# Local and summary attention with two dense layers on one core: queries and keys loaded as token pairs and turned by 64-column products with the identity

## Chip, cores and metric

One Trainium2 chip, one core of it. The metric is the device time of one launch in microseconds (us); lower is better. Before the change: 624.55 us, the median of three runs (623.58 to 625.62).

## What is computed

An attention over 2 batches, 8 heads, 768 tokens and 64 dimensions, in float32, whose result is the input of two dense layers. Cut to what matters:

```python
k_sum = k.reshape(B, H, nb, 32, D).max(axis=3)      # maximum over blocks of 32 tokens
v_sum = v.reshape(B, H, nb, 32, D).mean(axis=3)
scores_l = scale * q @ k.T, masked to |i - j| < 16
scores_s = scale * q @ k_sum.T + log(32)
a = softmax(concat(scores_l, scores_s))
x = a @ concat(v, v_sum)                             # then (B*S, H*D) = (1536, 512)
x = softplus(x @ w1_in) @ w1_out                     # 512 -> 2048 -> 512
out = relu(x @ w2_in) ** 2 @ w2_out
```

## The kernel before

**Tiling.** The tokens are cut into 12 tiles of 128, six of each batch. For a tile the kernel needs the queries and keys with the head dimension on the partitions: `qT` and `kT` hold two heads on the 128 partitions (head 2p on 0 to 63, head 2p+1 on 64 to 127), four such pairs and then the tokens. They come from `ld_qk` (line 336), which loads a unit of 256 tokens, all heads, with tokens on the partitions, and `tr` (line 344), which turns it. A unit is two halves r of 128 tokens. For each half there is one load of 256 KB, one PSUM bank that takes four transposes of 128x128 (one for each pair of heads, line 351), a copy of the bank to `kT` or `qT` by ACT or DVE (lines 296 and 298), and for keys a maximum by DVE from the same bank into `ks` (line 359). There are 3 units of keys and 3 of queries in a batch, so 24 loads and 24 banks in all. The word bank is used below for such a filled bank and its work.

**Attention of a tile.** POOL copies the 96 keys of a window behind the 24 block maxima (`kaug`, line 411), PE forms the scores (line 443, 64x64 corners of the array), DVE, ACT and POOL do the softmax, PE transposes the weights (line 499) and multiplies by the values (line 513, products with 64 columns and 120 rows of weights); two passes split the result into `xh` and `xl` (lines 522 and 523). The block means of the values are a product with a selection matrix (line 391, 24 columns).

**Dense layers.** All products are of float32 split in a high and a low part: three products each (lines 616 and 653). The first four of 16 chunks of the first layer are done during the attention, in steps of 256 tokens ("phase A", 24 steps); all else follows in steps of 512 tokens ("phase B"). Weights come as 64-bit floats and are put together by ACT, DVE and POOL (lines 561 to 575) in four places `raw`.

**Order.** `Plan.run` (line 86) simulates the program with the costs that each `op` carries and writes out the order of the instructions of every engine. `kb` is the price of a load on the queue of the DMAs. Where it sees PE idle it inserts products of the identity with itself (line 809, the function `warm`). On the chip each engine goes through its list in order.

```python
op("SP", 0.6, due, load, w=[(place, r)], kb=288)
op("PE", 0.66, due, mm, r=["id", (place, r)], w=[bk], take=bk)
op(("ACT", "DVE"), (0.62, 0.8), due, cp, r=[bk], give=bk, ...)
```

All loads are issued from SP, in one list: queries, keys, values, windows of values (line 377) and weights (lines 551 and 554).

Of the kernel before, what the change touches and what calls it, by code (L numbers as in the profile page):

```python
# [13 lines left out]
ALU = mybir.AluOpType  # L14
AX = mybir.AxisListType
# [163 lines left out]
def kernel(  # L179
# [54 lines left out]
    ident = ac.tile([128, 128], F32, name="ident")  # L234
# [7 lines left out]
    kT = ac.tile([128, NP, S + 32], F32, name="kT")  # L242
    ks = ac.tile([128, NP, NS], F32, name="ks")
    sel = ac.tile([128, VR, NS], F32, name="sel")
    vsum = ac.tile([NS, H * D], F32, name="vsum")
    qT = [ac.tile([128, NP, 256], F32, name=f"qT{i}") for i in range(2)]
    kaug = [ac.tile([128, NP, 2, NC], F32, name=f"kaug{i}") for i in range(2)]
# [6 lines left out]
    ab = [ps_a.tile([128, 512], F32, name=f"ab{i}") for i in range(2)] + hb[0:2]  # L254

    def st4(t):
        return t.rearrange("p (r h d) -> p r h d", h=H, d=D)

    pf = [part[i].rearrange("p a b -> p (a b)") for i in range(NB3)]
    PL = {("P", i, j): st4(pf[i][:, 1024 * j:1024 * j + 1024]) for i in range(NB3) for j in range(2)}  # L260
# [7 lines left out]
    for L in (1, 2):  # L268
        for ph, (f0, f1) in enumerate(PH):
            A = L == 1 and ph == 0  # L270
            n = 256 if A else 512
# [18 lines left out]
    def tt(e):  # L290
        return nc.gpsimd if e == "POOL" else nc.vector

    def copy(e, out_, in_, mul=None):

        if e == "ACT":
            nc.scalar.activation(out=out_, in_=in_, func=AF.Copy, **({} if mul is None else {"scale": mul}))  # L296
        else:
            tt(e).tensor_scalar(out=out_, in0=in_, scalar1=1.0 if mul is None else mul, scalar2=1.0,  # L298
                                op0=ALU.mult, op1=ALU.mult)
# [33 lines left out]
            nc.vector.memset(vwin[i], 0.0)  # L333


    def ld_qk(src, u, place, due):
        b, i = divmod(u, NU)
        for r in range(2):
            t0 = 256 * i + 128 * r
            op("SP", 0.6, due, lambda r=r, t0=t0: nc.sync.dma_start(  # L340
                out=PL[place][:, r], in_=src[b, :, t0:t0 + 128, :].rearrange("h t d -> t h d")),
                w=[(place, r)], kb=288)

    def tr(src, u, place, due):
        i = u % NU
        for r in range(2):
            bk = Bank()

            def mm(r=r, bk=bk):
                for p in range(NP):  # L350
                    nc.tensor.transpose(ab[bk.bank][:, 128 * p:128 * p + 128],
                                        PL[place][:, r, 2 * p:2 * p + 2].rearrange("t h d -> t (h d)"), ident)

            def cp(e, r=r, bk=bk):
                o = kT[:, :, 16 + 256 * i:16 + 256 * i + 256] if src is k else qT[u % 2]
                copy(e, o[:, :, 128 * r:128 * r + 128], ab[bk.bank].rearrange("p (a c) -> p a c", a=NP), None if src is k else scale)

            def kmax(r=r, bk=bk):
                nc.vector.tensor_reduce(out=ks[:, :, 8 * i + 4 * r:8 * i + 4 * r + 4],  # L359
                                        in_=ab[bk.bank].rearrange("p (a n t) -> p a n t", a=NP, t=32), op=ALU.max, axis=AX.X)  # L360

            op("PE", 0.66, due, mm, r=["id", (place, r)], w=[bk], take=bk)
            op(("ACT", "DVE"), (0.62, 0.8), due, cp, r=[bk], give=bk, w=[("kT", 2 * i + r)] if src is k else [("qT", u % 2, r)])
            if src is k:
                op("DVE", 0.67, due, kmax, r=[bk], give=bk, w=[("ks", 2 * i + r)])

    def ksum(x, due):
        op("DVE", 0.35, due, lambda: nc.vector.tensor_copy(
            out=kaug[x][:, :, :, 0:NS], in_=ks.rearrange("p a (o n) -> p a o n", o=1).to_broadcast([128, NP, 2, NS])),
            r=[("ks", i) for i in range(NTB)], w=[("kaug", x)])  # L370

    def ld_win(t, due):
        b, i = divmod(t, NTB)
# [32 lines left out]
    def mk_kaug(t, due):  # L406
        i = t % NTB
        for j in range(2):
            c0 = 128 * i + 64 * j
            us = sorted({min(max((c0 + d - 16) // 128, 0), NTB - 1) for d in (0, 95)})  # L410
            op("POOL", 0.55, due, lambda j=j, c0=c0: nc.gpsimd.tensor_scalar(
                out=kaug[t % 2][:, :, j, NS:], in0=kT[:, :, c0:c0 + WIN],
                scalar1=1.0, scalar2=1.0, op0=ALU.mult, op1=ALU.mult),
                r=["z"] + [("kT", u) for u in us], w=[("kw", t % 2, j)])

    def tile_sc(t, due):
        x, i, u = t % 2, t % NTB, (t // 2) % 2
# [4 lines left out]
        pe_mask = style in "mn"  # L422
# [5 lines left out]
        def scv(hh):  # L428
            return scb[:, hh, 0:NP * NC].rearrange("p (a c) -> p a c", a=NP)

        def mm():
            if pe_mask:
                for hh in range(2):
                    nc.tensor.matmul(out=scv(hh), lhsT=identb, rhs=maskb[:, var:var + 1].to_broadcast([128, NP, NC]),
                                     start=True, stop=False, skip_group_check=True)
                    for j in range(2):
                        nc.tensor.matmul(out=scv(hh)[:, :, 0:NS], lhsT=identb,
                                         rhs=logb[:, j:j + 1].to_broadcast([128, NP, NS]),
                                         start=False, stop=False, skip_group_check=True)
            for p in range(NP):  # L440
                for hh, j in ((0, 0), (1, 1), (0, 1), (1, 0)):
                    o = 128 * x + 64 * j
                    nc.tensor.matmul(out=scb[64 * j:64 * j + 64, hh, NC * p:NC * p + NC],  # L443
                                     lhsT=qT[u][64 * hh:64 * hh + 64, p, o:o + 64],
                                     rhs=kaug[x][64 * hh:64 * hh + 64, p, j], start=not pe_mask, stop=True,
                                     skip_group_check=pe_mask)
        op("PE", 1.7 if pe_mask else 1.15, due, mm, r=[("qT", u, x), ("kaug", x), ("kw", x, 0), ("kw", x, 1), "id"],
           w=[(sck, 0), (sck, 1)])
        if not pe_mask:
            for hh in range(2):  # L450
                op("DVE", 0.66, due, lambda hh=hh: nc.vector.tensor_tensor(  # L451
                    out=st[:, NP * hh:NP * hh + NP], in0=scv(hh),
                    in1=mask[:, var:var + 1].to_broadcast([128, NP, NC]), op=ALU.add),
                    r=[(sck, hh), "id"], w=[("s", y, hh)])
        halves = ((0, NP), (NP, H)) if t < 2 or pe_mask else ((0, H),)
        for h0, h1 in halves:
            n = (h1 - h0) / H
            hh = h0 // NP
# [12 lines left out]
            if pe_mask:  # L471
                op("DVE", 1.25 * n, due, lambda hh=hh, mv=mv: nc.vector.tensor_reduce(
                    out=mv, in_=scv(hh), op=ALU.max, axis=AX.X, negate=True), r=[(sck, hh)], w=mk)

                def exps(hh=hh, sv=sv, mv=mv, rv=rv):
# [4 lines left out]
                   w=sk + (rk if style == "n" else []), tab="exp")  # L480
            else:
                op("DVE", 1.25 * n, due, lambda sv=sv, mv=mv: nc.vector.tensor_reduce(out=mv, in_=sv, op=ALU.max, axis=AX.X),
                   r=sk, w=mk)
                op(("POOL", "DVE"), (1.8 * n + 0.1, 1.75 * n), due, lambda e, sv=sv, mv=mv, spread=spread: tt(e).tensor_tensor(
                    out=sv, in0=sv, in1=spread(mv), op=ALU.subtract), r=mk, w=sk)
# [3 lines left out]
                out=sv, in0=sv, in1=spread(rv), op=ALU.mult), r=rk, w=sk)  # L489
# [354 lines left out]
```

## Time and profile before

| | us |
|---|---|
| median of the runs | 624.55 |
| lowest, highest | 623.58, 625.62 |
| the profiled execution, its time | 623.45 |
| its span in the profile | 621.7 |
| PE busy | 601.9 |
| DVE, ACT, POOL busy | 309.6, 288.1, 201.2 |

The profile is of one execution. A record of PE is a product (MATMUL) or a load of the stationary operand (LDWEIGHTS); records overlap, so the distance from start to start is the time that an instruction takes from the engine, and the length of a record is longer. A float32 product leaves two MATMUL records, a transpose one. The column PEclk is the clock of TensorE that was granted: 1.00 stands for 2.4 GHz and 0.50 for 1.2 GHz. In the view by stages, "PE busy (x)" is the busy time and the number of instructions. In the timeline the parts are start, length, engine, line, operation, output and inputs, sizes, count, and in brackets the idle time ahead of it and what ended it.

### The profile page before, as it was taken

To read this page: it belongs to the slowest core of one execution; us is meant where nothing else is said; L and a number is where in the kernel's file an instruction comes from. 1 tells how busy PE (TensorE), PEld (TensorE's weight loads), DVE (VectorE), ACT (ScalarE), POOL (GpSimd) and SP (SyncE) were. 2 spreads that over 40 slices of the span, in tenths; PEclk is the share of its full clock that TensorE was granted. 3 is DMA by queue.
4 is the path that set the end of the run, shared out by engine and by line. 5 is a ranking of instruction groups with operands and counts; after the bars stand their busy time and mean duration, and the time that the engine had idled before them with its cause. 6 is when DMAs were issued, how large, how long until landed. Compare 5 with 4: busy or idle time off the path is not lost.

```text
span 621.7 us, 9362 instructions
## 1 busy us (share of the span) xinstructions
PE 601.9 (97%) x3751; PEld 505.4 (81%) x3751; DVE 309.6 (50%) x453; ACT 288.1 (46%) x512; POOL 201.2 (32%) x200
## 2 busy tenths in 40 slices
PE   7887899999999999999999999999999999999997
PEld 5776789999888888888888888888888888888885
DVE  4786898845754133742226752248432533242332
ACT  4776896775763225543337643356312332212220
POOL 4766776435750033411228540135000320000000
PEclk8999999999999999999999999999999999999999
DMA  9999722133550023430014430124000200010011
GB/s 214 270 263 265 189 52 58 55 93 114 166 182 14 1 68 102 135 103 0 1 34 130 143 101 1 34 97 126 16 0 1 68 2 0 1 51 18 17 52 67
DMA packets 68620, 51.33 MB, mean 83 GB/s; under 512 B 44512, under 2 KB 62944, under 8 KB 68576
## 3 DMA queue, kind: packets, MB, share of 16 engines
q1 hardware_dynamic: 68576, 50.73, 29.0%
q8 instruction: 29, 0.48, 0.3%
q14 instruction: 15, 0.12, 0.1%
HBM read 47.58 MB, written 3.15 MB: 82 GB/s over the span
## 4 chain that ended last, share of the span: by engine, by line
PE 85%; DVE 6%; DMA 4%; ACT 2%; SPq 2%; issue 0%; POOL 0%; DVEq 0%; ACTq 0%
PE h L616 41%; PE accp L653 23%; PE acc L653 18%; DMA raw<-in_moe_w_in_dram 2%; DMA late<-in_v_dram 2%; DVE raw L566 2%; SPq L340 1%; PE ab L513 1%; PE ab L499 1%; DVE sm L468 1%; ACT at L296 0%; DVE wil L575 0%; PE sc L443 0%; DVE ks L359 0%; DVE s L451 0%; DVE xl L523 0%
## 5 line engine op out<-in xcount | busy, mean ns | idle before, releaser
L616 PE MATMUL h<-xh,wih 128*128 128x512 f32 (+1 forms) x432 | 160.0, 370 | 0.5 <-DVE g1l L632 0.5
L616 PE MATMUL h<-xl,wih 128*128 128x512 f32 (+1 forms) x432 | 158.8, 368 | 1.1 <-DVE xl L523 1.1
L616 PE MATMUL h<-xh,wil 128*128 128x512 f32 (+1 forms) x432 | 158.8, 368 | 0.0
L566 DVE SCALAR_TENSOR_TENSOR raw<-raw 128x512 uint32<-128x512 uint32 x128 | 115.8, 923 | 47.6 <-ACT raw L561 28.2
L616 PEld LDWEIGHTS h<-xh,wih 128*128 128x128 f32 x432 | 81.4, 188 | 15.2 <-DVE g1l L632 0.9
L616 PEld LDWEIGHTS h<-xl,wih 128*128 128x128 f32 x432 | 81.3, 188 | 14.9 <-DVE xl L523 1.3
L616 PEld LDWEIGHTS h<-xh,wil 128*128 128x128 f32 x432 | 81.3, 188 | 14.0
L625 ACT ACTIVATE e<-h 128x512 f32<-128x512 f32 x48 | 28.7, 597 | 128.5 <-PE h L616 128.5
L627 DVE SCALAR_TENSOR_TENSOR h<-h,e 128x512 f32<-128x512 f32 x48 | 33.5, 698 | 107.2 <-ACT e L625 107.2
L623 ACT ACTIVATE h<-h 128x512 f32<-128x512 f32 (+1 forms) x60 | 29.7, 498 | 83.1 <-PE h L616 82.9
L298 POOL TENSOR_SCALAR wih<-raw 128x512 fp32r<-128x512 f32 x20 | 14.0, 701 | 153.2 <-PE h L616 143.9
L575 POOL TENSOR_TENSOR wol<-raw,woh 128x512 fp32r<-128x512 f32 x31 | 44.7, 1444 | 32.2 <-ACT woh L296 31.7
L561 ACT ACTIVATE raw<-raw 128x512 uint32<-128x512 uint16 x62 | 41.6, 674 | 17.5 <-DMA raw<-in_moe_w_out_dram 8.1
L575 POOL TENSOR_TENSOR wil<-raw,wih 128x512 fp32r<-128x512 f32 x31 | 42.0, 1353 | 22.8 <-ACT wih L296 21.3
L632 DVE TENSOR_TENSOR g1l<-h,g1h 128x512 fp32r<-128x512 f32 (+1 forms) x40 | 24.2, 607 | 33.9 <-ACT g1h L630 33.8
L675 DVE TENSOR_TENSOR part<-accp,part 128x512 f32<-128x512 f32 x24 | 16.0, 686 | 44.9 <-PE accp L653 44.9
L632 DVE TENSOR_TENSOR g2l<-h,g2h 128x512 fp32r<-128x512 f32 x28 | 19.3, 689 | 35.9 <-ACT g2h L630 35.7
L296 ACT ACTIVATE raw<-raw 128x512 f32<-128x512 f32 x41 | 27.5, 671 | 19.9 <-DVE raw L566 19.9
L632 DVE TENSOR_TENSOR g0l<-h,g0h 128x512 fp32r<-128x512 f32 (+1 forms) x40 | 24.1, 603 | 21.8 <-ACT g0h L630 21.6
L298 POOL TENSOR_SCALAR raw<-raw 128x512 f32<-128x512 f32 x23 | 18.8, 824 | 31.8 <-DVE raw L566 29.7
L630 ACT ACTIVATE g0h<-h 128x512 fp32r<-128x512 f32 (+1 forms) x40 | 21.4, 535 | 15.8 <-DVE h L627 15.4
L488 POOL TENSOR_TENSOR s<-s,sm 128x480 f32<-128x480 f32 (+1 forms) x16 | 22.9, 1435 | 16.2 <-DVE sm L470 12.6
(174 smaller groups left out, 1162.9 us busy)
## 6 DMA issues: line engine op xcount, KB each, us to landing
raw<-in_moe_w_in_dram SPq DMA_DIRECT2D x32, 512.0 KB, 4.4
raw<-in_moe_w_out_dram SPq DMA_DIRECT2D x32, 512.0 KB, 3.5
vwin<-in_v_dram SPq DMA_DIRECT2D x20, 192.0 KB, 4.2
part<-in_k_dram SPq DMA_DIRECT2D x12, 256.0 KB, 5.0
late<-in_v_dram SPq DMA_DIRECT2D x2, 1536.0 KB, 10.5
out_dram<-part SPq DMA_DIRECT2D x12, 256.0 KB, 2.2
part<-in_q_dram SPq DMA_DIRECT2D x10, 256.0 KB, 5.2
vwin<-in_v_dram SPq DMA_DIRECT2D x4, 160.0 KB, 5.1
```

The lines of the kernel that those rows point to most:

```text
L296: nc.scalar.activation(out=out_, in_=in_, func=AF.Copy, **({} if mul is None else {"scale": mul}))
L298: tt(e).tensor_scalar(out=out_, in0=in_, scalar1=1.0 if mul is None else mul, scalar2=1.0, op0=ALU.mult, op1=ALU.mult)
L488: op(("POOL", "DVE"), (1.8 * n + 0.1, 1.75 * n), due, lambda e, sv=sv, rv=rv, spread=spread: tt(e).tensor_tensor(out=sv, in0=sv, in1=sprea ...
L561: nc.scalar.activation(out=lo, in_=q4[:, :, 1], func=AF.Copy, scale=2.0 ** -13, bias=-4095.5 / 8192.0)
L566: nc.vector.scalar_tensor_tensor(out=lo, in0=hi, scalar=n, in1=lo, op0=how, op1=ALU.bitwise_or)
L575: op(("POOL", "DVE"), (1.4, 1.0), dv, lambda e: tt(e).tensor_tensor(out=ws[s][kl], in0=lo.bitcast(F32), in1=ws[s][kh].bitcast(F32), op=ALU ...
L616: nc.tensor.matmul(out=hview(st), lhsT=ws[s][wn][:, w_], rhs=xx[bl][:, kk, o:o + n], start=(kk == 0 and xx is xh and wn == "ih"), stop=(kk ...
L623: op("ACT", ta, due, lambda: nc.scalar.activation(out=hview(st), in_=hview(st), func=AF.Softplus), w=[H_], tab="sp")
L625: op("ACT", ta, due, lambda: nc.scalar.activation(out=e_t[st["g"] % 2], in_=hview(st), func=AF.Relu), r=[H_], w=[("e", st["g"] % 2)])
L627: op("DVE", tv, due, lambda: nc.vector.scalar_tensor_tensor(out=hview(st), in0=hview(st), scalar=0.0, in1=e_t[st["g"] % 2], op0=ALU.max, o ...
L632: op("DVE", tv, due, lambda: nc.vector.tensor_tensor(out=gview(st)[1], in0=hview(st), in1=gview(st)[0].bitcast(F32), op=ALU.subtract), r=[ ...
L653: nc.tensor.matmul(out=o, lhsT=a[:, sl], rhs=b, start=(st["first"] and c == 0 and not (A and m % 2)), stop=(st["last"] and c == 2 and not ...
```

## The change

A load now takes four of the eight heads (index z) and all 256 tokens of a unit, with tokens 2p and 2p+1 on partition p, so that 512 bytes in a row go to a partition where it was 256 bytes. The count (24) and size (256 KB) of the loads stay. PE turns a half z by eight products whose stationary operand is 64 columns of the data (one head, one of the two tokens) and whose moving operand is the identity of 128 columns; a head goes to partitions 0 to 63 or 64 to 127 of the bank. The copy out of the bank puts even and odd tokens back in turn (output in steps of two elements), and the maximum runs over two axes. The keys by which `Plan` tracks who waits for whom are now units and halves of the heads, not blocks of 128 tokens. The price `kb` of a load goes from 288 to 180; that of the PE step stays 0.66.

```diff
     def st4(t):
-        return t.rearrange("p (r h d) -> p r h d", h=H, d=D)
+        return t.rearrange("p (z a x) -> p z a x", z=2, a=NP)
...
     def ld_qk(src, u, place, due):
         b, i = divmod(u, NU)
-        for r in range(2):
-            t0 = 256 * i + 128 * r
-            op("SP", 0.6, due, lambda r=r, t0=t0: nc.sync.dma_start(
-                out=PL[place][:, r], in_=src[b, :, t0:t0 + 128, :].rearrange("h t d -> t h d")),
-                w=[(place, r)], kb=288)
+        for z in range(2):
+            op("SP", 0.6, due, lambda z=z: nc.sync.dma_start(
+                out=PL[place][:, z].rearrange("p a (r d) -> p a r d", r=2),
+                in_=src[b, 4 * z:4 * z + 4, 256 * i:256 * i + 256, :].rearrange("h (p r) d -> p h r d", r=2)),
+                w=[(place, z)], kb=180)
...
-                for p in range(NP):
-                    nc.tensor.transpose(ab[bk.bank][:, 128 * p:128 * p + 128],
-                                        PL[place][:, r, 2 * p:2 * p + 2].rearrange("t h d -> t (h d)"), ident)
+                for a in range(2):
+                    for r in range(2):
+                        for hh in range(2):
+                            o = 256 * a + 128 * r
+                            nc.tensor.matmul(out=ab[bk.bank][64 * hh:64 * hh + 64, o:o + 128],
+                                             lhsT=PL[place][:, z, 2 * a + hh, 64 * r:64 * r + 64], rhs=ident,
+                                             start=True, stop=True)
...
-                copy(e, o[:, :, 128 * r:128 * r + 128], ab[bk.bank].rearrange("p (a c) -> p a c", a=NP), None if src is k else scale)
+                copy(e, o[:, 2 * z:2 * z + 2].rearrange("p a (c r) -> p a r c", r=2),
+                     ab[bk.bank].rearrange("p (a r c) -> p a r c", a=2, r=2), None if src is k else scale)
...
-                nc.vector.tensor_reduce(out=ks[:, :, 8 * i + 4 * r:8 * i + 4 * r + 4],
-                                        in_=ab[bk.bank].rearrange("p (a n t) -> p a n t", a=NP, t=32), op=ALU.max, axis=AX.X)
+                nc.vector.tensor_reduce(out=ks[:, 2 * z:2 * z + 2, 8 * i:8 * i + 8],
+                                        in_=ab[bk.bank].rearrange("p (a r n c) -> p a n r c", a=2, r=2, n=8), op=ALU.max, axis=AX.XY)
...
-            us = sorted({min(max((c0 + d - 16) // 128, 0), NTB - 1) for d in (0, 95)})
+            us = sorted({min(max((c0 + d - 16) // 256, 0), NU - 1) for d in (0, 95)})
...
-        op("PE", 1.7 if pe_mask else 1.15, due, mm, r=[("qT", u, x), ("kaug", x), ("kw", x, 0), ("kw", x, 1), "id"],
+        op("PE", 1.7 if pe_mask else 1.15, due, mm, r=[("qT", u, 0), ("qT", u, 1), ("kaug", x), ("kw", x, 0), ("kw", x, 1), "id"],
```

Since `Plan.run` sees other prices and keys, the lists of all engines change in phase A; from the first step of phase B on PE's list is the same. The products of `warm` (line 809) go from 79 to 52. Lines behind the changed functions stand 7 lower in the file after the change.

On PE, at the start of the program: the first banks of keys (`part_68`, `part_69` are the places that the loads fill; `ab` and `h` are PSUM banks). Before:

```order
L351 MATMUL ab_141<-ident,part_68 128x128 x4
L351 MATMUL ab_142<-ident,part_68 128x128 x4
L351 MATMUL h_108<-ident,part_68 128x128 x4
L351 MATMUL h_109<-ident,part_68 128x128 x4
L351 MATMUL ab_141<-ident,part_69 128x128 x4
```

and after:

```order
L356 MATMUL ab_141<-ident,part_68 64x128 x8
L356 MATMUL ab_142<-ident,part_68 64x128 x8
L356 MATMUL h_108<-ident,part_68 64x128 x8
L356 MATMUL h_109<-ident,part_68 64x128 x8
L356 MATMUL ab_141<-ident,part_69 64x128 x8
```

The order is the same; each bank takes eight products in place of four transposes.

On PE, where the weights of the first two tiles are multiplied by the values (`vwin`) and the second unit of queries (`late`) is turned. Before:

```order
L351 MATMUL ab_142<-ident,late 128x128 x4
L513 MATMUL h_108<-at_134,vwin_130 64x64 x16
L513 MATMUL h_109<-at_135,vwin_131 64x64 x16
L351 MATMUL ab_141<-ident,late 128x128 x4
```

and after:

```order
L356 MATMUL ab_142<-ident,late 64x128 x8
L520 MATMUL h_108<-at_134,vwin_130 64x64 x16
L356 MATMUL ab_141<-ident,late 64x128 x8
L520 MATMUL h_109<-at_135,vwin_131 64x64 x16
L356 MATMUL ab_142<-ident,part_70 64x128 x8
```

Here banks stand between products that also have 64 columns; at other places they stand between products of 128 columns.

On SP, the loads from the 21st row of its list on (`part_70` from `in_k_dram` is the fifth unit of keys, `raw_77` from `in_moe_w_in_dram` the input weights of the fourth chunk). Before:

```order
L377 DMA vwin_131<-in_v_dram 96x8x64 x2
L340 DMA part_70<-in_k_dram 128x8x64
L551 DMA raw_77<-in_moe_w_in_dram 128x4x256
L340 DMA part_70<-in_k_dram 128x8x64
L554 DMA raw_78<-in_moe_w_out_dram 128x1024
```

and after:

```order
L384 DMA vwin_131<-in_v_dram 96x8x64 x2
L558 DMA raw_77<-in_moe_w_in_dram 128x4x256
L341 DMA part_70<-in_k_dram 128x4x128 x2
L561 DMA raw_78<-in_moe_w_out_dram 128x1024
```

The load of the weights moved ahead of one load of keys.

## Rows read from the trace of the kernel before

**Rows 1.** The page, part 1: busy time of each engine.
```profile
PE 601.9 (97%) x3751; PEld 505.4 (81%) x3751; DVE 309.6 (50%) x453; ACT 288.1 (46%) x512; POOL 201.2 (32%) x200
```

**Rows 2.** Stages: us, then PE, PEld, DVE, ACT, POOL busy, PEclk, DMA share, GB/s.
```profile
50.00:60.00 10.00, 6.61 (x137) 5.32 (x136) 6.45 (x12) 7.15 (x16) 5.76 (x8) 1.00 1.10 259
...
90.00:100.00 10.00, 9.04 (x119) 8.43 (x120) 9.93 (x16) 5.43 (x12) 7.24 (x7) 1.00 0.17 40
...
151.00:600.00 449.00, 449.00 (x1989) 369.92 (x1988) 193.63 (x268) 178.83 (x307) 108.26 (x91) 1.00 0.18 59
```

**Rows 3.** The page, below part 2: packets of the DMA engines by size.
```profile
DMA packets 68620, 51.33 MB, mean 83 GB/s; under 512 B 44512, under 2 KB 62944, under 8 KB 68576
```

**Rows 4.** Stages, as rows 2: loads of keys; the slow clock; the load of values.
```profile
2.00:9.00 7.00, 5.26 (x28) 3.40 (x25) 3.12 (x5) 1.99 (x5) 6.11 (x19) 1.00 1.19 222
9.40:16.00 6.60, 6.31 (x46) 4.81 (x50) 3.19 (x6) 3.35 (x7) 0.00 (x0) 0.50 1.09 272
18.00:20.00 2.00, 2.00 (x26) 1.69 (x19) 1.74 (x4) 2.00 (x9) 0.98 (x2) 1.00 1.08 397
```

**Rows 5.** Timeline of PE, the start: first and last banks, scores of tiles 0 and 1.
```profile
4.17 1.06 PE L351 MATMUL ab<-ident,part 128*128 128x128 f32 x4
...
11.86 1.94 PE L351 MATMUL h<-ident,part 128*128 128x128 f32 x8
...
14.85 1.68 PE L443 MATMUL sc<-kaug,qT 64*64 64x120 f32 x32
...
17.14 1.05 PE L443 MATMUL accp<-kaug,qT 64*64 64x120 f32 x32
```

**Rows 6.** Timeline of PE: one 64-column group and one bank among 128-column products.
```profile
29.82 2.08 PE L513 MATMUL h<-at,vwin 120*64 120x64 f32 x64
...
53.70 1.51 PE L391 MATMUL ab<-late,sel 128*24 128x128 f32 x48
...
61.65 0.28 PE L653 MATMUL accp<-g1l,woh 128*128 128x256 f32 x1
61.86 1.15 PE L513 MATMUL ab<-at,vwin 120*64 120x64 f32 x32
...
63.16 0.28 PE L616 MATMUL h<-xl,wih 128*128 128x256 f32 x1
...
64.36 0.28 PE L616 MATMUL h<-xh,wil 128*128 128x256 f32 x1
64.48 0.60 PE L351 MATMUL ab<-ident,part 128*128 128x128 f32 x4
...
65.03 0.28 PE L616 MATMUL h<-xl,wih 128*128 128x256 f32 x1
```

**Rows 7.** Timeline of PE, 25 to 73 us: waits and inserted products of the identity.
```profile
25.05 1.51 PE L391 MATMUL ab<-late,sel 128*24 128x128 f32 x48 [1.62 <-DMA late<-in_v_dram]
...
39.23 0.66 PE L351 MATMUL ab<-ident,part 128*128 128x128 f32 x4 [0.86 <-DVE ks L359]
...
55.15 0.72 PE L809 MATMUL h<-ident 128*128 128x256 bf16 x5
58.34 1.05 PE L443 MATMUL sc<-kaug,qT 64*64 64x120 f32 x32 [2.47 <-DVE s L451]
...
68.29 1.69 PE L809 MATMUL sc<-ident 128*128 128x256 bf16 x14
...
72.55 1.05 PE L443 MATMUL sc<-kaug,qT 64*64 64x120 f32 x32 [1.00 <-DVE kaug L368]
```

**Rows 8.** The chain that ended last, and the timeline of ACT, at 55 us.
```profile
47.78 7.58 DMA raw<-in_moe_w_in_dram
...
55.44 0.69 ACT L561 ACTIVATE raw<-raw 128x512 uint32<-128x512 uint16 x1 [2.72 <-DMA raw<-in_moe_w_in_dram]
```

**Rows 9.** Groups by line and shape, ACT: copies out of a bank, and a strided pass.
```profile
L561 ACT ACTIVATE raw<-raw 128x512 uint32<-128x512 uint16 x62 | 41.6, 674 | 17.5 <-DMA raw<-in_moe_w_out_dram 8.1 <-DMA raw<-in_moe_w_in_dram 7.6 <-DVE s L451 1.7
...
L296 ACT ACTIVATE kT<-ab 128x512 f32<-128x512 f32 x9 | 5.4, 598 | 7.2 <-PE ab L351 7.2
```

More of the change, by code (lines that the diff above doesn't have):

```diff
@@ L344, in tr, with mm, cp, kmax @@
     def tr(src, u, place, due):
         i = u % NU
-        for r in range(2):
+        for z in range(2):
             bk = Bank()
-            def mm(r=r, bk=bk):
-                for p in range(NP):
-                    nc.tensor.transpose(ab[bk.bank][:, 128 * p:128 * p + 128],
-                                        PL[place][:, r, 2 * p:2 * p + 2].rearrange("t h d -> t (h d)"), ident)
-            def cp(e, r=r, bk=bk):
-                o = kT[:, :, 16 + 256 * i:16 + 256 * i + 256] if src is k else qT[u % 2]
-                copy(e, o[:, :, 128 * r:128 * r + 128], ab[bk.bank].rearrange("p (a c) -> p a c", a=NP), None if src is k else scale)
-            def kmax(r=r, bk=bk):
-                nc.vector.tensor_reduce(out=ks[:, :, 8 * i + 4 * r:8 * i + 4 * r + 4],
-                                        in_=ab[bk.bank].rearrange("p (a n t) -> p a n t", a=NP, t=32), op=ALU.max, axis=AX.X)
-            op("PE", 0.66, due, mm, r=["id", (place, r)], w=[bk], take=bk)
-            op(("ACT", "DVE"), (0.62, 0.8), due, cp, r=[bk], give=bk, w=[("kT", 2 * i + r)] if src is k else [("qT", u % 2, r)])
+            def mm(z=z, bk=bk):
+                for a in range(2):
[5 more added lines that the diff above has]
+                                             start=True, stop=True)
+            def cp(e, z=z, bk=bk):
+                o = kT[:, :, 16 + 256 * i:16 + 256 * i + 256] if src is k else qT[u % 2]
+                copy(e, o[:, 2 * z:2 * z + 2].rearrange("p a (c r) -> p a r c", r=2),
+                     ab[bk.bank].rearrange("p (a r c) -> p a r c", a=2, r=2), None if src is k else scale)
+            def kmax(z=z, bk=bk):
+                nc.vector.tensor_reduce(out=ks[:, 2 * z:2 * z + 2, 8 * i:8 * i + 8],
+                                        in_=ab[bk.bank].rearrange("p (a r n c) -> p a n r c", a=2, r=2, n=8), op=ALU.max, axis=AX.XY)
+            op("PE", 0.66, due, mm, r=["id", (place, z)], w=[bk], take=bk)
+            op(("ACT", "DVE"), (0.62, 0.8), due, cp, r=[bk], give=bk, w=[("kT", i, z)] if src is k else [("qT", u % 2, z)])
@@ L364, in tr @@
             if src is k:
-                op("DVE", 0.67, due, kmax, r=[bk], give=bk, w=[("ks", 2 * i + r)])
+                op("DVE", 0.67, due, kmax, r=[bk], give=bk, w=[("ks", i, z)])
     def ksum(x, due):
@@ L369, in ksum @@
             out=kaug[x][:, :, :, 0:NS], in_=ks.rearrange("p a (o n) -> p a o n", o=1).to_broadcast([128, NP, 2, NS])),
-            r=[("ks", i) for i in range(NTB)], w=[("kaug", x)])
+            r=[("ks", i, z) for i in range(NU) for z in range(2)], w=[("kaug", x)])
     def ld_win(t, due):
@@ L413, in mk_kaug @@
                 scalar1=1.0, scalar2=1.0, op0=ALU.mult, op1=ALU.mult),
-                r=["z"] + [("kT", u) for u in us], w=[("kw", t % 2, j)])
+                r=["z"] + [("kT", u, z) for u in us for z in range(2)], w=[("kw", t % 2, j)])
     def tile_sc(t, due):
```

## The prediction

> **What bounds the kernel now.** I read the page first. PE is busy 97% of the span [rows 1], but that is an average over two stages. The view by stages shows them: from 151 to 600 us PE has no free moment (449.00 of 449.00 us), while between 50 and 60 us it is busy 6.61 of 10 us and the DMA engines are at 1.10, full [rows 2]. From 151 us on PE's list is unchanged, so the change is worth exactly what it moves the end of phase A. Phase A has limits in turn. Up to about 72 us the loads set the pace; at 90 to 100 us DVE is busy 9.93 of 10 us [rows 2]; behind that PE is full. A lead or a lag of PE's backlog at 72 us is therefore carried to the end, if DVE is not given more work. Then I read PE's timeline up to 73 us: its groups [rows 5, 6] and its waits [rows 7].
>
> **The loads.** Of 68,620 packets 44,512 are under 512 bytes [rows 3]. A load of keys or queries, 256 KB, is by the code 1024 pieces of 256 bytes. Alone on the queue such loads run at 222 GB/s [rows 4]: 262,144 bytes take 1.18 us. The values come in pieces of 1536 bytes at 397 GB/s [rows 4]. With 16 engines that is 18.4 ns and 61.9 ns for a piece; on the straight line between them 512 bytes take 27 ns, 302 GB/s, 0.87 us for a load. No row has this size, so this is an estimate; the ends are 1.18 us (nothing gained) and 0.66 us (the rate of the values). The nearest row is that of 256 bytes, so I take 0.87: 0.31 us saved on each of 24 loads, 7.4 us of a full queue.
>
> **The turning on PE.** Four transposes: from the last product ahead (64.36) to the second one behind (65.03) are 0.67 us, less two products of 0.12 (64.36 to 64.48) is 0.43 us for a bank [rows 6]. The eight products leave 16 records. Line 513 has the same form, 64 columns in two halves of the array: 32 more records cost 2.08 - 1.15 = 0.93 us, 29 ns each for 64 moving columns, so 58 ns for 128 [rows 6]. Line 391 moves 128 columns in four parts of the array: (1.51 - 0.28) / 48 = 26 ns [rows 6], so 51 ns in two parts. I take 55 ns between these ends: 0.88 us for a bank, 0.45 us more. At the slow clock both double.
>
> A change of width costs too. From 61.65 to 63.16 are 1.51 us [rows 6]; less two products of 0.12 and 0.93 us of records, 0.34 us stay, where the transposes leave none. In the list after, the 16 banks behind the start stand in twelve stretches, and six of those are alone among 128-column products; the others lean on groups that are 64 columns or narrower already. I count six times 0.3.
>
> So the 16 later banks add 16 x 0.45 + 6 x 0.3 = 9.0 us to PE. The Trainium skill, *TensorEngine Tiling (Array Packing)*, Key Properties, says that changing the tiling mode drains TensorE, which speaks against this change. The trace agrees, with the 0.34 us above. By that rule all twelve stretches would pay.
>
> **The start.** Before, the first bank begins at 4.17, the eighth (second half of the x8 group at 11.86) at about 12.7, and tiles 0 and 1 are scored from 14.85 and 17.14 [rows 5], at half clock: PEclk is 0.50 (1.2 GHz) from 9.40 to 16.00, while PE did short groups of transposes with waits for loads [rows 4]. The mask products between the end of the eighth bank (12.7 + 0.86) and 14.85 took 1.3 us at that clock. After, loads come every 0.87 us, so the eighth lands near 10. PE is now the later one: first bank at 3.9, at the slow clock (as the 1.06 us of the first group shows) 1.76 us, to 5.7; then seven banks at full clock with a hand-over, 0.9 us each, to 12.0; mask products half of 1.3, 0.65 us. Tile 0 is scored from 12.65; a group of scores is 1.05 us long at full clock [rows 5], with masks 1.7, so tile 1 begins at 14.35: **2.8 us earlier**. This takes the clock as staying at 2.4 GHz, since PE is no longer idle between banks. At 1.2 GHz from 9.4 us on, 3.6 us of that are lost.
>
> **From 25 to 73 us.** Here the 9.0 us must fit. PE's timeline has eleven bracketed waits, from 1.62 us at 25.05 to 1.00 us at 72.55, in sum 9.8 us, and 19 inserted products of the identity (at 55.15 and 68.29) of 2.4 us, 12.2 us in all [rows 7]. The largest, 2.47 us at 58.34 and the inserted work ahead of it, goes back to one load: input weights in flight from 47.78 for 7.58 us, for which ACT waited 2.72 us with the softplus queued behind it on ACT [rows 8]. That load gains 18 x 0.31 us from the loads ahead, and 1.2 us more since it moves past one of them in SP's list: it lands near 48.6, and is no longer last. What stays is what no load sets: four waits on the maximum of a bank and on the softmax (0.86 us at 39.23 is one [rows 7]), 2.9 us, and I add 1.1 us for new waits, because a bank is held 0.45 us longer and there are two banks. So 12.2 - 2.9 - 1.1 = 8.2 us of the 9.0 are covered. If that cover is gone they are all paid.
>
> **What costs nothing.** The copies write in steps of two elements: 598 ns now, 674 ns for a pass of ACT that steps in this way [rows 9], so at most 0.08 us x 24, on an engine with a quarter of its time free here; I take none. The maximum over two axes reads the same 512 elements; twice the time at worst would be 12 x 0.7 us on DVE, and nothing excludes a small loss; I take none. Coarser units make nobody wait: the last reader of a unit of keys stands well ahead of its next writer in the lists, and scores need the maxima of all keys anyway. DVE takes over one split of weights and one shift and gives up two copies, at 40 to 57 us, where it has gaps (6.45 of 10 us busy [rows 2]). The stretch from 70 to 100 us where DVE is full has the same work.
>
> **Sum.** -2.8 + 9.0 - 8.2 = **-2.0 us**. The profiled execution is 623.45 us, 1.1 below the median, so I apply the difference to the median: 624.55 - 2.0 = **622.5 us**. By the skill's rule for all twelve stretches: 2 us more.
>
> **Rivals.**
> - *PE becomes the bound before 73 us* (slower). Only the wait that a load made, 3.2 us with its filler, is covered, and the other latencies stay, since they come from DVE, ACT and POOL between two steps of PE. Then -2.8 + 9.0 - 3.2 = +3.0: 627.5. It turns the sign when less than 6.2 us are covered. For it: 2.9 us of waits are of this kind by their releasers. Against it: phase A has 24 steps of the dense layer as filler. 30%.
> - *All of it is covered.* The waits vanish with the earlier loads: -2.8 + 9.0 - 12.2 = -6.0: 618.5. For it: the DMA engines are full until 72 us, and most chains start at a load. 18%.
> - *Every stretch pays for its change of width*: 12 x 0.34 in place of 1.8 is +2.3: 624.8. For it: the 0.34 us. Against it: neighbours of like width in the list. 8%. (The Trainium skill's rule on modes, named above, would have it so.)
> - *The clock falls at the start as before*: -2.0 + 3.6: 626.1. For it: it did so with the same eight banks. Against it: PE has no gaps now. 5%.
> - *The loads are no faster* (the change does not do what it says): the eighth bank lands at 12.4, tile 1 gains 1.6 us instead of 2.8, and 2 us of the stall at 55 stay: -1.6 + 9.0 - 6.2 = +1.2: 625.7. For it: no row has 512-byte pieces. Against it: larger pieces go faster in all rows. 5%.
>
> **How the numbers follow.** The forecast has 34%, its own range is 621 to 624. A measurement can tell a difference of 0.3%, 1.9 us. The forecast lies at that bound; I give 22 points of it to faster and 12 to the same. Faster: 22 + 18 = 40%. Same: 12 + 8 + 5 + 5 = 30%. Slower: 30%. The range reaches from the case with everything covered to just past the one with PE as the bound: 618.5 to 628.5.
>
> **What would show it.** Loads: 256 KB in 0.87 us each, and under 512 bytes some 19,900 packets (44,512 less 24,576). PE: 192 products in 384 records of line 356; a bank of 0.88 us, and 0.3 us around lone ones. Start: PEclk 1.00 from 6 us on, scores of tile 0 at 12.7 and of tile 1 at 14.4. Middle: no wait for DMA at 55 us, the first score of the second batch (72.55 before) at 70.5. Phase B begins at 149.3 in place of 151.3, and PE is full from there. I am wrong if PE's waits in 25 to 73 us stay above 6 us, if tile 1 is scored after 16 us, or if DVE's full stretch lasts beyond 98 us.

## The result, and the profile after

The change made the kernel slower: 629.68 us in the median of six runs (629.03 to 631.05) beside 624.32 for the kernel before (six runs, 623.58 to 625.62). The ratio is 1.0086, with a 95% interval of 1.0072 to 1.0101. The forecast was 622.5, so its sign was wrong and the time lies 1.2 us above its range. The profiled execution took 629.45 us, its span is 627.3.

The page of the kernel after, busy time of the engines and the line of packets, against [rows 1, 3]:

```profile
PE 611.1 (97%) x4012; PEld 516.1 (82%) x4012; DVE 308.9 (49%) x453; ACT 293.3 (47%) x518; POOL 199.9 (32%) x194
...
DMA packets 56333, 51.36 MB, mean 82 GB/s; under 512 B 19936, under 2 KB 50656, under 8 KB 56288
```

PE is busy 9.2 us longer, and 24,576 packets of less than 512 bytes are gone, as many as the 24 loads of 1024 pieces have.

Stages of the kernel after, columns as in rows 2 (PE, PEld, DVE, ACT, POOL busy, PEclk, DMA share, GB/s):

```profile
2.00:9.00 7.00, 7.00 (x90) 6.18 (x88) 3.12 (x5) 2.60 (x5) 5.66 (x18) 1.00 1.03 279
9.40:16.00 6.60, 6.44 (x127) 5.16 (x124) 5.09 (x10) 5.22 (x11) 1.87 (x5) 1.00 1.05 361
...
24.00:30.00 6.00, 6.00 (x111) 5.41 (x103) 2.67 (x4) 4.81 (x12) 4.78 (x6) 0.84 1.05 284
40.00:50.00 10.00, 5.42 (x96) 4.37 (x98) 3.67 (x8) 4.64 (x8) 4.45 (x7) 0.82 1.23 213
...
50.00:60.00 10.00, 10.00 (x128) 9.07 (x124) 6.14 (x14) 6.33 (x16) 4.60 (x6) 0.84 1.06 263
90.00:100.00 10.00, 8.89 (x139) 7.83 (x139) 9.90 (x15) 7.53 (x12) 9.26 (x8) 1.00 0.18 41
100.00:110.00 10.00, 8.01 (x80) 7.65 (x79) 7.73 (x12) 7.43 (x13) 8.04 (x7) 0.83 0.36 93
...
156.60:600.00 443.40, 443.38 (x1961) 365.04 (x1961) 193.68 (x268) 180.16 (x310) 108.52 (x90) 1.00 0.19 60
```

The start is as forecast: loads at 279 GB/s where 222 were seen, and PEclk 1.00 where it was 0.50 [rows 4]. Behind 156.6 us PE is full, as before [rows 2]. The damage is in 40 to 50 us: PE is busy 5.42 us of 10, and DVE and ACT stand still for more than half of it too (3.67 and 4.64 us busy, where it was 8.22 and 7.54 before), while the DMA engines are full. PEclk is below 1.00 in four of these stages; before, it was so at the start alone.

PE's timeline of the kernel after, against [rows 5 to 7]:

```profile
3.88 2.73 PE L356 MATMUL ab<-ident,part 128*64 128x128 f32 x32
...
9.94 1.93 PE L356 MATMUL h<-ident,part 128*64 128x128 f32 x32
12.48 1.05 PE L450 MATMUL sc<-kaug,qT 64*64 64x120 f32 x32
14.14 1.05 PE L450 MATMUL accp<-kaug,qT 64*64 64x120 f32 x32
...
22.40 2.69 PE L398 MATMUL ab<-late,sel 128*24 128x128 f32 x48 [2.21 <-DMA late<-in_v_dram]
...
44.04 0.34 PE L520 MATMUL ab<-at,vwin 120*64 120x64 f32 x4 [0.60 <-DMA vwin<-in_v_dram]
45.03 1.03 PE L520 MATMUL ab<-at,vwin 120*64 120x64 f32 x28 [0.66 <-DMA vwin<-in_v_dram]
...
54.87 0.28 PE L660 MATMUL accp<-g0l,woh 128*128 128x256 f32 x1
55.07 1.97 PE L356 MATMUL ab<-ident,part 128*64 128x128 f32 x32
56.97 0.39 PE L660 MATMUL accp<-g0h,woh 128*128 128x256 f32 x1
...
75.97 1.05 PE L450 MATMUL sc<-kaug,qT 64*64 64x120 f32 x32
...
104.28 0.44 PE L623 MATMUL h<-xh,wih 128*128 128x256 f32 x1 [1.99 <-DVE g0l L639]
...
156.54 0.40 PE L623 MATMUL h<-xh,wih 128*128 128x512 f32 x1
```

The last row is the first product of phase B. It stood at 151.33 before, so 5.2 us were lost ahead of it, and that is nearly the whole result (5.4 us between the medians). The scores of tile 1 are 3.0 us earlier than in [rows 5]; those of tile 6 (75.97) are 3.4 us later than the 72.55 of [rows 7]. The other 1.8 us were lost behind tile 6, around the wait of 1.99 us at 104.28.

PE's account up to phase B is an estimate, worked out by giving each product its start-to-start time at 2.4 GHz (for example 0.12 us for 256 columns); "clock" is what the same products took longer at 1.2 GHz, "nothing" the rest, changes of width included:

| | products | clock | inserted products | nothing | sum, us |
|---|---|---|---|---|---|
| before | 111.7 | 3.6 | 10.0 | 26.0 | 151.3 |
| after | 122.1 | 6.5 | 6.9 | 21.1 | 156.5 |

PE got 10.4 us more to do, and 8.0 us of that went into time that had been empty or filled. The clock gave nothing back, since the lower level left the start and came at three other places (0.84, 0.82 and 0.83 above), each during a wait or right behind one: 2.21 us at 22.40, 3.07 at 49.14, 1.99 at 104.28. The stages in which it was low, columns as above:

```profile
22.60:25.90 3.30, 3.30 (x52) 2.82 (x45) 2.68 (x4) 0.74 (x3) 2.36 (x2) 0.50 0.95 231
46.50:53.20 6.70, 4.06 (x26) 3.73 (x27) 3.00 (x6) 3.67 (x8) 0.65 (x1) 0.50 1.11 298
104.50:107.80 3.30, 3.30 (x17) 3.30 (x17) 2.75 (x5) 2.38 (x4) 2.49 (x4) 0.50 0.46 104
```

The second began 0.4 us into its wait, which started at 46.07. PE was busy for 10.7 us of the three; at 2.4 GHz that work takes half, so the clock cost some 5.3 us here (an estimate).

What stood still in 46 to 49 us, from the timeline of all engines of the kernel after:

```profile
47.20 0.65 ACT L568 ACTIVATE raw<-raw 128x512 uint32<-128x512 uint16 x1 [4.15 <-DMA raw<-in_moe_w_out_dram]
...
47.76 0.60 ACT L296 ACTIVATE kT<-ab 128x512 f32<-128x512 f32 x1
...
48.39 0.69 DVE L366 TENSOR_REDUCE ks<-ab 128x16 f32<-128x512 f32 x1 [6.17 <-ACT kT L296]
...
49.14 1.12 PE L356 MATMUL ab<-ident,part 128*64 128x128 f32 x8 [3.07 <-DVE ks L366]
```

ACT waited 4.15 us for output weights. Behind the waiting instruction in its list stood the copy of a bank of keys that PE had filled at 42.35 to 43.4. The maximum by DVE comes after that copy and PE's next bank after the maximum, so three engines waited for one load that none of them needed at that moment.

### The profile page after: what moved, and what is told of

Its sections match the earlier page's. It is cut to its first block, busy times and chain, and to the rows that moved or that the text cites. A ratio compares the mean times of both kernels' runs of the same rounds, so it can differ in the third digit from the quotient of the medians.

```text
span 627.3 us, 9879 instructions
## 1 busy us (share of the span) xinstructions
PE 611.1 (97%) x4012; PEld 516.1 (82%) x4012; DVE 308.9 (49%) x453; ACT 293.3 (47%) x518; POOL 199.9 (32%) x194
## 4 chain that ended last, share of the span: by engine, by line
PE 87%; DVE 6%; DMA 3%; POOL 1%; ACT 1%; issue 1%; DVEq 0%; POOLq 0%; ACTq 0%
PE h L623 41%; PE accp L660 23%; PE acc L660 18%; DMA raw<-in_moe_w_out_dram 2%; PE ab L356 2%; DVE raw L573 2%; DVE sm L475 1%; PE ab L520 1%; DMA raw<-in_moe_w_in_dram 1%; PE ab L506 1%; DVE sm L476 1%; PE sc L450 1%; PE h L356 1%; DVE mx L489 1%; DVE s L458 0%
## 5 line engine op out<-in xcount | busy, mean ns | idle before, releaser
L573 DVE SCALAR_TENSOR_TENSOR raw<-raw 128x512 uint32<-128x512 uint32 x128 | 113.9, 907 | 35.1 <-ACT raw L568 23.6
L298 POOL TENSOR_SCALAR wih<-raw 128x512 fp32r<-128x512 f32 x17 | 12.6, 742 | 130.9 <-PE h L623 126.7
L296 ACT ACTIVATE raw<-raw 128x512 f32<-128x512 f32 x44 | 29.4, 673 | 15.6 <-DVE raw L573 15.6
L637 ACT ACTIVATE g1h<-h 128x512 fp32r<-128x512 f32 (+1 forms) x40 | 21.4, 535 | 9.5 <-DVE h L634 9.1
```

The lines of the kernel that those rows point to most:

```text
L573: nc.vector.scalar_tensor_tensor(out=lo, in0=hi, scalar=n, in1=lo, op0=how, op1=ALU.bitwise_or)
L637: op("ACT", ta, due, lambda: nc.scalar.activation(out=gview(st)[0], in_=hview(st), func=AF.Copy), r=[H_] + need, w=gk[0])
```

## The experiments

Theory A: `Plan.run` writes the lists for loads that take kb/245 us, 0.73 us with kb = 180. On the chip they take longer, so instructions that need a load stand ahead of ready work. Theory B: the added work of PE itself. Theory C: any rewritten list moves the time, whatever the prices. Ratios are to the kernel before, on the same chip.

**One split of weights moved (e_move).** The lists of PE, POOL and SP stay; on ACT the split moves as shown, and on DVE the step that needs it (line 573) moves with it, behind the second bank's maximum:

```diff
-L568 raw (split of the output weights)
 L296 kT
 L637 g0h
 L296 xh
 L296 kT
+L568 raw
```

> The kernel after, with one step put later in two lists: the split of the output weights on ACT (which waited 4.15 us for its load until 47.20) and the DVE step that hangs on it stand behind the second bank of keys' copy and maximum instead of ahead of the first. All else is the same. Theory A (the lists were written for loads that land 5 to 9 us earlier than they do, so that a wait for a load stands ahead of work that is ready): the bank that began at 49.14 begins near 46.1, the 3.07 us wait ahead of it is gone, and 2 to 4 us of the loss come back, 626 to 628. Theory B (the 10.4 us of added PE work cannot be hidden, whatever the lists): less than 1 us, 629 to 630.

Measured: 626.27 us, ratio 1.0011 (0.9998 to 1.0025). The loss went from 0.86% to 0.11%, so this one wait was worth 0.75%, 4.7 us (3.5 to 5.9 with both intervals): more than its 3.07 us. Its timeline at the same place:

```profile
44.02 1.09 PE L356 MATMUL ab<-ident,part 128*64 128x128 f32 x16
...
45.22 0.63 ACT L296 ACTIVATE kT<-ab 128x512 f32<-128x512 f32 x1 [0.60 <-PE ab L356]
...
45.89 0.69 DVE L366 TENSOR_REDUCE ks<-ab 128x16 f32<-128x512 f32 x1 [2.01 <-ACT kT L296]
...
47.79 1.05 PE L356 MATMUL ab<-ident,part 128*64 128x128 f32 x16
...
49.40 0.66 ACT L568 ACTIVATE raw<-raw 128x512 uint32<-128x512 uint16 x1
```

The copy follows its bank, PE's next bank at 47.79 has no wait, and the split runs at 49.40 without one. Theory A holds here. This profiled execution, 628.15 us, was the slowest of its twelve. PE's list is the same as in the kernel after, product for product, so the two profiles can be laid side by side. PE came to this place 1.9 us later than in the kernel after, since its values had come later (3.09 us of wait at 24.17). It was 1.3 us earlier at the second bank (47.79 for 49.14) and 3.2 us earlier by 53: the place gave back 5.1 us, 3.2 by the wait and 1.9 by the clock, which was at 2.4 GHz here (PEclk 1.00 from 40 to 60 us). Smaller waits between 55 and 65 us took 1.9 us of it again.

**Less work for PE under the same lists (e_half).**

```diff
-    8 x nc.tensor.matmul(out=ab[..64 rows..], lhsT=PL[place][:, z, 2 * a + hh, 64 * r:64 * r + 64], rhs=ident, ...)
+    4 x nc.tensor.transpose(ab[bk.bank][:, 128 * h:128 * h + 128], PL[place][:, z, h], ident)
```

> The kernel after, with the eight products of a bank replaced by four transposes of 128 columns (a head's two tokens at once); the lists stay as they are and PE has 10 us less work. What it leaves out: heads and tokens come out in a wrong place in kT and qT, so the scores are not the reference's; every bank is filled as before. Theory A (late loads set the waits): most of the PE time saved turns into waits for the same loads, 626 to 629. Theory B (PE's added work is the loss): 619 to 622.

Measured: 629.80 us, ratio 1.0081 (1.0058 to 1.0104), as slow as the change. Ten microseconds less work on PE bought nothing, and the same chain stands there, as its timeline of all engines shows:

```profile
46.79 0.65 ACT L564 ACTIVATE raw<-raw 128x512 uint32<-128x512 uint16 x1 [4.55 <-DMA raw<-in_moe_w_out_dram]
...
48.73 1.11 PE L353 MATMUL ab<-ident,part 128*128 128x128 f32 x4 [3.31 <-DVE ks L362]
```

**More work for PE under the old lists (e_before64).**

```diff
-    nc.tensor.transpose(ab[..][:, 128 * p:128 * p + 128], PL[place][:, r, 2 * p:2 * p + 2], ident)
+    for hh in range(2):
+        nc.tensor.matmul(out=ab[..][64 * hh:64 * hh + 64, 128 * p:128 * p + 128],
+                         lhsT=PL[place][:, r, 2 * p + hh], rhs=ident, start=True, stop=True)
```

> The kernel before, loads and lists unchanged, with the four transposes of a bank replaced by eight products of 64 columns with the identity (0.44 us more on PE for each of 24 banks, 10.5 us in all). Theory A: the waits and inserted products of this list take most of it in, 625 to 628. Theory B: 632 to 635.

Measured: 626.47 us, ratio 1.0020 (1.0005 to 1.0036). All the added products cost 1.2 us, and theory B falls. But this is a net figure. At the start, with the loads of before, PE stayed at 2.4 GHz in 9.4 to 16 us where it had been at 1.2, and tiles 0 and 1 were scored earlier than the 14.85 and 17.14 of [rows 5]. The stage and the timeline of PE:

```profile
9.40:16.00 6.60, 6.25 (x110) 4.79 (x106) 3.63 (x8) 3.18 (x6) 0.46 (x2) 1.00 1.17 315
```

```profile
14.31 1.05 PE L444 MATMUL sc<-kaug,qT 64*64 64x120 f32 x32
15.97 1.05 PE L444 MATMUL accp<-kaug,qT 64*64 64x120 f32 x32
```

**Honest prices (e_honest).**

```diff
-    kb=180      op("PE", 0.66, ...)
+    kb=213      op("PE", 0.95, ...)
```

> The kernel after, planned with the prices that the trace shows: kb 213 (0.87 us a load) in place of 180 (0.73), and 0.95 us for a bank on PE in place of 0.66. Theory A: no list waits for a load that lands 5 us later than planned, 620 to 624. Theory B: 627 or more.

Measured: 628.50 us, ratio 1.0052 (1.0034 to 1.0070). It misses theory A's 620 to 624. The stall at 46 us is gone, but the plan drew another list, in which tile 6 is scored at 89.9 us. So theory A alone is not enough, and the two prices had to be taken apart.

**The price of loads alone, 213, 250, 288 and 340 (e_kb213, e_kb250, e_kb288, e_kb340).** Only kb differs from the kernel after.

> The kernel after with kb 213, the measured 0.87 us of a load, and the PE price left at 0.66. Theory A: lateness at 50 us of about 6 us, between that of kb 180 and of kb 288, and a time between them, 625 to 628. Theory C: anywhere from 621 to 632.

> The kernel after with kb 250, 1.02 us for a load that takes 0.87: between the two prices 213 (624.9 beside 624.9 of before) and 288 (623.6). Theory A: the lateness of loads at 50 us lies near 3 us and the time between those two, 623 to 625. Theory C (chance of the list): anywhere from 621 to 632.

> The kernel after, with the price of a load of keys or queries put back from kb 180 to 288 (0.73 to 1.18 us in the plan; on the chip such a load takes 0.87). Loads now land before the plan wants them. Theory A (the loss is that lists wait for loads that the plan thought landed): lateness of loads against the plan falls from 8 to 10 us to under 2 at 45 to 50 us, no wait for a load or behind one above 1 us from 30 to 60 us, 622 to 625. Theory C (any rewriting of the lists moves the time by half a per cent either way, whatever the prices): the time falls anywhere from 621 to 632 and does not follow the lateness.

> The kernel after with its loads priced at 340, as in e_before_kb340, so that both kernels are compared with lists that never wait for loads. Theory E (the change itself is worth about nothing: earlier loads and added PE work cancel): 621 to 624, no faster than e_before_kb340 (0.9947 of before). Theory F (the forecast's sum holds once the lists are right, 2 us and more below e_before_kb340): 618 to 620.

Measured: 624.89, 625.25, 623.62 and 623.05 us, ratios 1.0004 (0.9988 to 1.0019), 1.0001 (0.9987 to 1.0015), 0.9977 (0.9964 to 0.9989) and 0.9960 (0.9944 to 0.9976). The first two lie just outside the ranges that theory A gave (625 to 628 and 623 to 625), by 0.1 and 0.3 us, the third inside its 622 to 625; the fourth lies in the range of theory E and not of F. The dearer the loads are to the plan, the faster the kernel (213 and 250 alike); from 180 to 340 it is 1.3%, with the same loads and the same products. Stages of e_kb288 in which the kernel after had 5.42 us and a clock of 0.82:

```profile
40.00:50.00 10.00, 9.75 (x146) 8.35 (x144) 7.66 (x16) 8.27 (x17) 5.60 (x8) 1.00 0.92 223
50.00:60.00 10.00, 9.99 (x177) 8.77 (x175) 7.66 (x13) 7.97 (x18) 6.07 (x9) 1.00 1.01 280
```

**The same price in the kernel before, 180, 310 and 340 (e_before_kb180, e_before_kb310, e_before_kb340).** Nothing but this number changes there.

> The kernel before, loads and PE work unchanged, with the price of its loads lowered from kb 288 to 180, so that the plan believes them 0.45 us faster than they are. Theory A: by 50 us loads land 9 us or more behind the plan, instructions that need them stand ahead of ready ones, and it is slower by 3 to 9 us, 627 to 633, though nothing but a number of the plan was changed. Theory C: within 2 us of before as easily as not, with no relation to the lateness.

> The kernel before with its loads priced at 310, between 288 and 340. If the time follows the lateness of loads: 622 to 624. If the gain of e_before_kb340 was the luck of one list: anywhere from 621 to 630; the plan itself gives this list a later end than its neighbours (8 us behind kb 288), which speaks for the upper part.

> The kernel before with its loads priced at 340 in place of 288; on the chip its loads come 3 to 4 us later than the plan has them by 50 us. Theory A: with that lateness gone before gains as well, 621 to 623.5, so that what e_kb288 gained over before may be the plan's and not the larger pieces'. Rival: 3 us of lateness did no harm, 624 to 626.

Measured: 631.54 us, 1.0102 (1.0071 to 1.0132); 629.54, 1.0077 (1.0047 to 1.0106); 622.29, 0.9947 (0.9927 to 0.9968). With 180 the old kernel shows the fault of the new one, on another load, in its timeline of ACT and PE and in its stage (this execution, 628.21 us, was the fastest of its six):

```profile
41.33 0.67 ACT L561 ACTIVATE raw<-raw 128x512 uint32<-128x512 uint16 x1 [4.40 <-DMA raw<-in_moe_w_in_dram]
41.90 1.08 ACT L477 ACTIVATE s<-sc,mx 128x120 f32<-128x120 f32 x4
...
43.04 0.56 PE L434 MATMUL sc<-maskb,identb 128*128 128x480 bf16 x1 [4.31 <-ACT s L477]
```

```profile
40.00:50.00 10.00, 6.19 (x52) 4.86 (x51) 5.02 (x9) 6.63 (x15) 4.70 (x6) 0.59 1.16 302
```

So 180 and 340 came out as theory A said, although the list of 180 also scores tile 6 late, at 89.9 us, and its 1.0% is not the lateness alone. The price 310 stands between 288 and 340, is slower than both and misses the 622 to 624 of theory A. Theory C is partly right: its list scores tile 6 at 90.6 us, and its timeline of PE (of the slowest of its seven executions, 633.59 us) has these waits:

```profile
45.41 0.66 PE L351 MATMUL ab<-ident,part 128*128 128x128 f32 x4 [2.58 <-ACT at L296]
...
70.46 2.31 PE L809 MATMUL sc<-ident 128*128 128x256 bf16 x11 [2.15 <-DVE s L451]
```

How late loads were, against their price. For the 27th and the 38th load in SP's order it is the landing that the plan adds up (kb/245 each), against the end of the packets that carry these bytes, counted in order. Each row is one execution, and the counting is good to some 0.3 us; in e_move, with the list of SP and the prices of the kernel after, the two loads were 1.9 and 1.5 us later than in the row of the kernel after:

| kernel | kb | 27th, us late | 38th, us late | tile 6 scored at | ratio |
|---|---|---|---|---|---|
| after | 180 | 5.2 | 8.4 | 76.0 | 1.0086 |
| e_kb213 | 213 | 3.1 | 5.9 | 72.4 | 1.0004 |
| e_kb250 | 250 | -0.8 | 2.3 | 77.3 | 1.0001 |
| e_kb288 | 288 | -2.4 | -0.3 | 77.0 | 0.9977 |
| e_kb340 | 340 | -6.9 | -4.5 | 76.6 | 0.9960 |
| e_before_kb180 | 180 | 10.0 | 12.3 | 89.9 | 1.0102 |
| before | 288 | 3.0 | 3.6 | 72.5 | 1 |
| e_before_kb310 | 310 | 2.1 | 4.7 | 90.6 | 1.0077 |
| e_before_kb340 | 340 | -0.8 | 0.0 | 71.0 | 0.9947 |

Among lists with tile 6 near 71 to 77 us the time follows the lateness roughly. Lateness as such is not the cost: e_move, with loads as late as those of the kernel after or later, stands at 1.0011. The cost is the ready work that waits behind a load. A list with tile 6 near 90 us is slower than its lateness says, which holds for e_honest (4.5 us late, 1.0052) and the next one too. Why such a list loses was not taken apart.

**The price of PE's banks under loads that are in time (e_288pe88).**

```diff
-    kb=180      op("PE", 0.66, ...)
+    kb=288      op("PE", 0.88, ...)
```

> The kernel of e_kb288 with the bank on PE priced at 0.88 us, what the trace shows, in place of 0.66. Theory A: the price of PE's banks is of no account, since PE has spare time around them; 622 to 626. Theory D (the plan also loses by taking PE for faster than it is): 620 to 622. The plan itself writes the first scores of the second batch much later in this list, which speaks against a gain.

Measured: 626.91 us, ratio 1.0023 (1.0005 to 1.0040), tile 6 at 90.6 us. It lies above both expectations: the honest price did not help. The kernel is half a per cent slower than e_kb288, with the list that this price led to.

**PE's work under loads that are in time (e_half288, e_before64_340).** The edits of e_half and e_before64, on the kernels of e_kb288 and e_before_kb340.

> The kernel of e_kb288 (change, loads priced at 288), with four transposes of 128 columns in place of the eight products of a bank, as in e_half: PE has 10.5 us less work under a list that no longer waits for loads. What it leaves out: heads and tokens come out in a wrong place, so the scores are not the reference's. Theory A (waits of a few us and PE's spare time, not PE's work, set the end of phase A): within 2 us of e_kb288, 622 to 625. Theory B (PE's work counts as soon as the loads are in time): 615 to 619.

> The kernel of e_before_kb340 with the four transposes of a bank replaced by eight products of 64 columns: PE's added work alone, under a list that is on time. Theory E: 1 to 3 us above e_before_kb340, 623 to 626, since some of PE's spare time takes it in. Theory B (PE's work counts in full): 629 or more.

Measured: 622.24 us, 0.9951 (0.9932 to 0.9969), beside the 0.9977 of e_kb288; and 622.91, 0.9960 (0.9943 to 0.9977), beside the 0.9947 of e_before_kb340. The added products, 10.5 us, cost 1.6 us and 0.8 us at the end, the second within what can be told. Theory B (615 to 619, and 629 or more) misses both.

**The start alone (e_hyb288, e_hyb340).** The first eight banks as in the change, the other sixteen loaded and turned as before:

```diff
+    def pairs(src, u):
+        return u < NU if src is k else u == 0
```

> Only the first eight banks (keys of batch 1 and the first queries) use loads of token pairs and products of 64 columns; the other sixteen are loaded and turned as before; all at kb 288. PE has 7 us less work behind the start than with e_kb288, and 16 loads are slower by 0.31 us. Theory A: the start gains 1.5 to 2 us (tile 1 scored near 15), and loads stay on the plan: 621 to 624, the same as e_kb288 or up to 2 us slower than it. Theory B (PE's added work counts): 3 us or more below e_kb288.

> The first eight banks as in the change, the other sixteen as before, all loads priced at 340. The start gains up to 2.5 us at no cost on PE behind it. If the start's gain reaches the end, 1 to 2 us below e_kb340: 620 to 622; if it is lost in the waits that follow, 622 to 625.

Measured: 625.91 us, 1.0025 (1.0006 to 1.0044), and 623.40, 0.9970 (0.9952 to 0.9988). The lists are those of e_kb288 and e_kb340. At 288, with 7 us less work on PE and 16 slower loads, it is half a per cent slower than e_kb288 and outside the 621 to 624 of theory A, but theory B had it 3 us faster: by the count above its 38th load is 3.4 us late, where that of e_kb288 is not. At 340 the two cannot be told apart, and 623.40 lies where the start's gain is lost (622 to 625).

## Why the prediction was wrong, by its steps

**What bounds: right.** The end of phase A moved by 5.2 us and the time by 5.4; phase B is unchanged.

**The loads: right.** 0.87 us was the estimate; at 284 GB/s (24 to 30 us) 262,144 bytes take 0.92. The price that fits this is 226, so 213 was a little low too.

**The turning on PE: right for a bank, low for the changes of width.** Two banks in a row take 0.87 us longer than one, where 0.88 was forecast. From 54.87 to 56.97 are 2.10 us; less one product of 0.12 and two banks of 0.88 this leaves 0.22 for the changes of width, where 0.3 was counted. But they were counted at six of the twelve stretches of banks behind the start. In the trace of the kernel after, ten of the twelve have no wait in them; nine of these pay 0.13 to 0.33 us, also those that lean on narrow groups, and only the one between two groups of line 520 pays nothing (0.03). Their sum is 2.2 us, where 1.8 was counted for all twelve. So the rival in which every stretch pays was right in kind, while its price of 0.34 for each was too high. All this was no loss of its own: the added products cost 0.8 to 1.6 us at the end where loads are in time. The forecast's net of 9.0 - 8.2 = 0.8 is close to that by luck, since the 8.2 did not come about as forecast.

**The start: right in time, and without gain at the end.** Tiles 0 and 1 were scored at 12.48 and 14.14, where 12.65 and 14.35 were forecast, and the clock stayed at 2.4 GHz. Faster loads are not the only reason: with the old loads the added products alone brought 1.2 of the 3.0 us for tile 1 (e_before64). But the -2.8 us did not travel to the end. At tiles 2 and 3 (the kernel before first, then after) 0.75 and 0.5 us were left:

```profile
32.99 1.05 PE L443 MATMUL sc<-kaug,qT 64*64 64x120 f32 x32
40.39 0.84 PE L443 MATMUL sc<-kaug,qT 64*64 64x120 f32 x24
```

```profile
32.24 1.05 PE L450 MATMUL sc<-kaug,qT 64*64 64x120 f32 x32
39.88 1.05 PE L450 MATMUL sc<-kaug,qT 64*64 64x120 f32 x32
```

Some 1.7 us went to the clock at 22.6 us (half of the 3.3 us above). With loads in time in both, the whole change (0.9960) is no faster than the kernel before (0.9947), and the start alone gives 0.9970; as the lists differ, this does not show that the gain is nothing under every list.

**From 25 to 73 us: the step that failed**, 12.2 - 2.9 - 1.1 = 8.2, and with it the clock, for which the sum had nothing outside the start. In sum the waits fell nearly as forecast, to 4.6 us (0.25, 0.60, 0.66 and 3.07) where 4.0 were to be left, but they are other waits. The term of 1.1 us for new ones, "because a bank is held 0.45 us longer", is the one that was wrong, and so is the assumption under it that loads which land earlier end the waits for loads. The lists were rewritten too, for loads at 0.73 us, and moved forward by more than the loads did. A wait of 3.07 us came on PE behind 4.15 us on ACT for a load, the clock fell to 1.2 GHz with it, and e_move puts this one place at 4.7 us. Between the forecast (phase B 2.0 us earlier) and the result (5.2 us later) lie 7.2 us. The clock at the three places is some 5.3 of them by the estimate above; the waits behind tile 6, 3.1 us where it was 1.6, are another 1.5.

The prediction had the numbers for it. Its own 0.87 us beside the plan's 180/245 = 0.73 is 0.14 us for each of the first 18 such loads, 2.5 us of the 5.2 by which the 27th load was late (the kernel before was 3.0 late with its price of 1.18). It took its estimate for a gain and never laid it beside the plan's price.

**What costs nothing: mostly right.** The strided copy of keys takes 0.64 us in the mean (0.598 before), so 0.04 us more each, and the maximum 0.69 as before. DVE's full stretch lasted to 106 us, past the 98 that the prediction named as a sign of error; but in the kernel before it had already lasted to 103, so 98 was no fair sign.

**The rivals.** The slower one (627.5, 30%) had the sign and nearly the size, but not the mechanism: PE was not the bound, as e_half shows. No rival was about the order in the lists. The Trainium skill, *PSUM — Partial Sum Buffer*, Engine vs sequencer instructions, says that the queues of ScalarE, VectorE and GpSimd are strictly first in, first out. The trace agrees, with a ready copy held on ACT until a 4.15 us wait ahead of it was over.

**What beats both.** The kernel before with the single number kb = 340: 622.29 us, 0.9947 of before. The change with kb = 340 (623.05, 0.9960) also beats both, and the two cannot be told apart.

## What to carry to other kernels

When a planner writes the order, a change is two changes: the work, and the prices that rewrite every list. Compare each new price with the duration in the trace and add the difference up over the loads ahead in the queue; a price that is too low put waits ahead of ready work here, while one well too high (340) did no harm. Before trusting a change of half a per cent, run the old code under neighbouring prices, since a list alone moved this kernel by 1.5%.

## What was not expected of the hardware

More work on PE kept its clock up at the start: e_before64 differs from the kernel before in the added products alone, and has 1.00 in 9.4 to 16 us where that has 0.50. Further on more work was no guard: the clock fell during waits or right behind them, though not at each of them. In e_before_kb180 PE waited 4.31 us and the granted clock of 40 to 50 us was 0.59. The kernel after did 10.4 us more work than the one before and was at 1.2 GHz at three places with waits. e_kb288, with the same work, waited longer than the kernel after for the first values, and its stage had PEclk 1.00. Its timeline of PE and the stage:

```profile
23.84 1.51 PE L398 MATMUL ab<-late,sel 128*24 128x128 f32 x48 [3.10 <-DMA late<-in_v_dram]
```

```profile
20.00:30.00 10.00, 6.40 (x130) 5.70 (x131) 7.37 (x14) 6.94 (x17) 8.05 (x9) 1.00 1.02 205
```

In both kernels PE was at 2.4 GHz ahead of that wait, so what decides is not shown by these runs.

A load's last packets can come long after most of it. The 128 pieces of 4096 bytes of the output weights began between 41.4 and 45.9 us in the kernel after, half of them by 43.0, and ACT could start only at 47.20.
